# An attention stage of 24 steps, issued in the order of a table instead of step by step

## The chip, the cores and the metric

The kernel runs on one core of a Trainium2 chip. Five engines work side by side, each on its own queue of instructions and in the order of that queue: TensorE (PE in the profile; its weight loads are shown apart as PEld), VectorE (DVE), ScalarE (ACT), GpSimd (POOL) and SyncE (SP), which here issues nearly all transfers. The metric is the device time of one execution in microseconds (us); the figure for the kernel before is the median of three runs.

## The reference

Three blocks stand one behind the other. The first, on which the change works, is a linear attention with a forget gate, for 4 batches, 8 heads, 768 positions and a head size of 48:

```
f = 1 / (1 + exp(-f_logit))
for t in range(768):
    state = f[t][:, None] * state + outer(k[t], v[t])      # per batch and head, 48 x 48
    y[t]  = q[t] @ state
```

Its output, as 3072 tokens of 384 values, goes through a soft mixture of eight experts (logits against 32 slots, a softmax over tokens and one over slots, two matrices per expert with a relu between) and then through a gated block, `(sigmoid(x @ w_gate) * (x @ w_val)) @ w_out`.

## The kernel before

**Tiling.** The attention is worked in chunks of 128 positions: 6 chunks of 4 batches give 24 steps, and step i is chunk i // 4 of batch i % 4 with all eight heads (four lie side by side in the free dimension, two in the partitions). Within a step the forget gates are summed up in the logarithm, from the end of the chunk to its start, and keys and queries are scaled by the exponentials of the sums. Then scores, masked scores, output and state follow as matrix products.

**The operations of a step.** The names in brackets are those that the change's table uses, and this text uses them with the step or group behind a dot (A.4 is the scores of step 4).
- Gates, two steps together (group g holds steps 2g-1 and 2g): the transfer (F); a clamp on GpSimd (C, line 310); two activations on ScalarE, exp and ln (EX and LN, lines 314 and 315); per step the running sum, a scan on VectorE (S, line 319); two exponentials on ScalarE, with minus (E) and plus sign (R, both line 324).
- Keys and queries: one transfer for both (KQ, line 298) into one of three buffers `kq`; the key product in two halves (K, line 340) on GpSimd; the query product (Q, line 344), on GpSimd for odd steps from 3 on and on VectorE otherwise.
- State: the old one times the chunk's decay on GpSimd (SB, line 352, from step 4 on); the transposed keys by TensorE and their copy out of PSUM by ScalarE (KT and KTC, lines 156 and 157); the product of keys and values (KV, line 383) and its addition to the state on VectorE (ZA, lines 391 and 393). GG (line 350) keeps the gates' smallest values.
- Output: scores on TensorE (A, line 365); the masking on VectorE (M, line 372), which also brings them from PSUM to the one buffer `r`; query times old state (YI, line 401) and scores times values (YA, line 413) on TensorE; the copy out by ScalarE (Y, line 419).
- For the second block: the output transposed (XT, line 163) and copied (X, line 165). Once in four steps the logits of a chunk on TensorE (L), their maximum and a copy (D1), the exponentials on ScalarE (DD), a transposition (DT with the copies DTC and LNC), the running sum (SR), a product that sums up the slots' inputs (SIP, line 224) and its addition (ADD, line 233).
- For the third block: six pieces of `w_gate` and `w_val` are loaded as 64 bit numbers (RAW) and narrowed to fp32, by one ScalarE instruction (ABS, line 439) and four on VectorE (N1 to N4, lines 114 to 119), in steps 3, 6, 9, 12, 15 and 18. The experts' weights (W, 20 transfers of 768 KB, and W2) are spread over the steps by `load_weights`.

There is one PSUM buffer for the scores and one `r`, so A of a step waits for M of the step before, and M waits for YA of the step before. The buffers of keys and queries are three, so KQ.(i+3) can be issued when the last reader of step i is done.

**Order.** Nothing reorders the work: each engine takes the operations as the Python loop `for i in range(NSTEP)` issues them, with what must run ahead (gates, keys and queries of the next steps) written into the loop by hand. After the loop, a tail (from line 650) ends the last chunk, and the experts follow (`rest`).

Of the kernel before, what the change touches and what calls it, by code (L numbers as in the profile page):

```python
# [31 lines left out]
CONV_AT = 3, 6, 9, 12, 15, 18  # L32
NP2 = NSTEP // 2 + 1
LOAD_FROM, LOAD_TO = 1, NSTEP - 2
# [8 lines left out]
def body(ctx, tc, fd, kqd, v, phi, w1, w2, wg, wv, wo, out_t):  # L43
# [85 lines left out]
    def attention_in(att, aps, slow):  # L129
# [23 lines left out]
        def kt_stage(k, kts):  # L153
            ps = pt([128, HP, 112], "m", MB, "ktp")
            for h in range(HP):
                PE.transpose(ps[:, h], k[0:112, h], ident[0:112, 0:112])
            A.copy(heads_of(kts), heads_of(ps))

        def x_stage(i):
            yt = yts[i % 4]  # L160
            ps = pt([128, HP, 112], "m", MB, "xtp")
            for h in range(HP):
                PE.transpose(ps[:, h], yt[0:112, h], ident[0:112, 0:112])
            x = xt[i] = xs[i % 5]
            (V.tensor_copy if i == NSTEP - 1 else A.copy)(x, heads_of(ps))
# [37 lines left out]
        def d2(u):  # L203
            ps = pt([128, 2, T], "m", MB, "dtp")
            PE.transpose(ps[:, 0], dd, ident)
            if u < NU - 1:
                PE.transpose(ps[:, 1], ll, ident)
            A.copy(dt, ps[:, 0])
            if u < NU - 1:
                A.copy(lnat[:, u].rearrange("p b s -> p (b s)"), ps[:, 1])  # L210
# [31 lines left out]
        def fast_steps():  # L242
# [69 lines left out]
            def prep_a(g, k=None):  # L312
                w = part(g, k)
                A.activation(w, w, AF.Exp, scale=-1.0)
                A.activation(w, w, AF.Ln, bias=1.0)  # L315
# [5 lines left out]
            def prep_e(g, k=None):  # L321
                w = valid(g) if k is None else slice(k, k + 1)
                for t, sc in ((ee, -1.0), (rr, 1.0)):
                    A.activation(  # L324
                        t[g % 2][0:112, w, :, 0:T].rearrange("p k h t -> p (k h) t"),
                        part(g, k).rearrange("p (x t) -> p x t", t=T), AF.Exp, scale=sc,
                    )
# [18 lines left out]
            def z_stage(i, eng):  # L346
                g, k = at_step(i)
                if k == 1 or i == NSTEP - 1:
                    lo = max(2 * g - 1, 0)
                    eng.tensor_copy(gmin[0:112, lo:i + 1], ee[g % 2][0:112, valid(g), :, 0])  # L350
                if i >= B:
                    eng.tensor_tensor(
                        sb[i % 2][0:112], zs[i % B][0:112], decay(ee, i, 0, 1).to_broadcast([112, HP, D]),
                        op=ALU.mult,
                    )
# [15 lines left out]
            def m_stage():  # L371
# [58 lines left out]
            def load_raw(p):  # L430
                if 0 <= p < NP:
                    raws[p] = rawt[:, 0:2 * GW].rearrange("p (n w) -> p n w", w=2)
                    w, n = (wg, wv)[p // KC].bitcast(I32), 2 * GW
                    SP.dma_start(raws[p].rearrange("p n w -> p (n w)"), w[0][:, p % KC * n:(p % KC + 1) * n])

            def conv_a(i):
                if i in CONV_AT:
                    p = CONV_AT.index(i)
                    A.activation(piece(p), raws[p].bitcast(F32)[:, :, 1], AF.Abs)

            def conv(i):
                if i not in CONV_AT:
                    return [lambda: None] * 4
                p = CONV_AT.index(i)
                return narrow_steps(piece(p), raws[p])

            loads = [(768, lambda n=n: load_w1(*divmod(n, 2))) for n in range(E * 2)]
            loads += [
                (768, lambda e=e, h=h: load_w2(e, slice(4 * h, 4 * h + 4))) for e in range(2) for h in range(2)
            ]  # L450
            total, given = sum(n for n, _ in loads), [0]

            def load_weights(i, part):
                due = total * (i + part - LOAD_FROM) / (LOAD_TO - LOAD_FROM)
                while loads and given[0] < due:
                    n, f = loads.pop(0)
                    given[0] += n
                    f()

            def once(fn, i, *a):  # L460
                if 0 <= i < NSTEP:
                    fn(i, *a)

            load_f(0)
            load_f(1, 0)
            load_kq(0)
            load_phi(A)
            make_keep()
            load_f(1, 1)
            load_kq(1)  # L470
            load_v(0)
            load_f(2)
            load_v(1)
            load_kq(2)
            for t in ee + rr:
                V.memset(t[:, :, :, T:T + 1], 1.0)
            prep_c(0)
            prep_c(1, 0)
            make_identity(nc, ident)
            make_mask()  # L480
            prep_c(1, 1)
            prep_a(0)
            V.memset(aps_, 0.0)
            prep_s(0)
            prep_e(0)
            prep_a(1, 0)
            prep_k(0, V)
            prep_q(0, V)
            prep_s(1)
            V.memset(kvp[32:64], 0.0)  # L490
            PO.memset(ident0[:, 128:160], 0.0)
            for i in range(NSTEP):
                u, b = divmod(i, B)
                more = u < NU - 1
                even = i % 2 == 0
                cv = conv(i)

                if i == 0:
                    prep_e(1, 0)
                    z_stage(0, PO)  # L500
# [4 lines left out]
                if not even and (i + 5) // 2 < NP2:  # L505
                    prep_c((i + 5) // 2)
# [5 lines left out]
                if i >= 8 and b == 2 or i == 6:  # L512
                    d2b(u - 1)
                if i >= B:
                    y_inter(i)
                if i == 0:
                    kt_stage(kq[0][:, 0], kts)
                    V.memset(yps[32:64], 0.0)
                    prep_a(1, 1)
                    prep_c(2)  # L520
                once(load_kq, i + 3)
                once(load_v, i + 2)
                if i == 0:
                    load_f(3)
                if not even:
                    load_f((i + 7) // 2)
                load_raw(CONV_AT.index(i + 2) if i + 2 in CONV_AT else -1)
                load_weights(i, 0)
                if even and (i + 4) // 2 < NP2:
                    prep_a((i + 4) // 2)  # L530
                if not even or i == 0:
                    once(prep_q, i + 1, V)
                if i == 0:
                    prep_s(2)
                    prep_e(1, 1)
                if not even and (i + 3) // 2 < NP2:
                    prep_e((i + 3) // 2)

                if more:
                    kv(i)  # L540
                    z_add(i)
                if i:
                    x_stage(i - 1)
                if i + 1 < NSTEP - B:
                    kt_stage(kq[(i + 1) % 3][:, 0], kts)
                if even:
                    once(prep_s, i + 3)
                if i >= 4 and b == 0:
                    l_stage(u - 1)
                    d1(u - 1)  # L550
                if i >= 4 and b == 1:
                    d2(u - 1)
                    d1b(u - 1)
# [5 lines left out]
                if i >= 4 and b == 0:  # L559
                    d1e(u - 1)  # L560
                if i == NSTEP - 3:
                    constants()
                if i == NSTEP - 2:
                    load_w2(2, slice(0, 8))

        def slow_steps():
# [8 lines left out]
            def slow_step(i):  # L575
# [11 lines left out]
                kt_stage(kk, kts)  # L587
# [44 lines left out]
            for i in range(NSTEP):  # L632
# [4 lines left out]
                x_stage(i)  # L637
                if i % B == B - 1:
# [3 lines left out]
                    d2(u)  # L642
                    d1b(u)
# [9 lines left out]
        x_stage(NSTEP - 1)  # L653
        d1e(u)
# [6 lines left out]
        d2(u)  # L661
        t2 = pt([128, 1], "a1" if slow else "kv", name="t2")
# [402 lines left out]
```

## Time and profile before

| what | value |
|---|---|
| median of 3 runs | 385.44 us (385.29 to 385.81) |
| the profiled execution | 384.68 us, span of the core 382.9 us |
| busy in the span | PE 88%, VectorE 64%, ScalarE 55%, GpSimd 54% |
| attention, first score product to the tail | 9.27 to 138.25 us |

The span is the core's own time in the trace; every time of a row is counted from its start. The shares are means over stages with different limits: the attention uses all five engines and the transfer queue, while in the last 200 us TensorE works nearly alone at its limit. What the change does is to be read from the first 140 us. TensorE's times are modelled, because its products overlap, so a mean of a group on PE is longer than what one adds to the queue; starts can be compared.

### The profile page before, as it was taken

How to read it: one execution, taken by the hardware profiler on the slowest of the kernel's cores; microseconds unless marked ns; L12 is line 12 of the kernel's file. 1: busy time of each engine (PE TensorE's matmuls, PEld its weight loads, DVE VectorE, ACT ScalarE, POOL GpSimd, SP SyncE). 2: the span in 40 equal slices, each digit the busy share in tenths (PEclk: the TensorE clock that was granted, in tenths of full speed). 3: DMA queues.
4: the chain of work that ended last, by engine and by line, in shares of the span. 5: the costliest groups of instructions: out<-in, count | busy, mean ns of one | idle time of the engine just before them, and what ended most of it. 6: DMA issues, size and time to landing. Idle time of an engine off the chain costs nothing.

```text
span 382.9 us, 8428 instructions
## 1 busy us (share of the span) xinstructions
PE 338.7 (88%) x3406; PEld 258.0 (67%) x3406; DVE 246.9 (64%) x407; ACT 209.3 (55%) x373; POOL 207.2 (54%) x200
## 2 busy tenths in 40 slices
PE   0796969888896989995879999999999999999993
PEld 0685758676675664453558886788887887888882
DVE  5678886878888646435767765547786566444442
ACT  5676755677784421134366665666555565444440
POOL 5596855777786400002466564666555566545550
PEclk9999997999997899998699999999999999999998
DMA  7679996999997969992001240030000000222222
GB/s 265 223 243 364 360 398 228 364 391 352 386 386 258 355 231 368 415 429 109 0 0 49 118 164 3 14 153 0 0 2 1 0 2 0 82 85 82 82 85 92
DMA packets 17456, 68.33 MB, mean 178 GB/s; under 512 B 1936, under 2 KB 5376, under 8 KB 15744
## 3 DMA queue, kind: packets, MB, share of 16 engines
q1 hardware_dynamic: 17280, 67.64, 46.8%
q8 instruction: 29, 0.48, 0.5%
q14 instruction: 19, 0.16, 0.1%
q10 hardware_dynamic: 128, 0.06, 0.1%
HBM read 62.97 MB, written 4.72 MB: 177 GB/s over the span
## 4 chain that ended last, share of the span: by engine, by line


## 5 line engine op out<-in xcount | busy, mean ns | idle before, releaser
L910 POOL TENSOR_TENSOR hl<-sg,hh 128x512 fp32r<-128x512 f32 x72 | 100.8, 1400 | 77.1 <-ACT hh L908 73.6
L906 DVE TENSOR_TENSOR sg<-sg,gvp 128x512 f32<-128x512 f32 x72 | 49.5, 687 | 69.2 <-ACT sg L905 69.0
L938 PE MATMUL oup<-hh,wo 128*128 128x512 f32 x216 | 85.8, 397 | 1.4 <-ACT acc L920 1.2
L939 PE MATMUL oup<-hh,wo 128*128 128x512 f32 x216 | 84.8, 393 | 0.0
L908 ACT CAST hh<-sg 128x512 fp32r<-128x512 f32 x72 | 44.8, 622 | 55.1 <-DVE sg L906 55.1
L340 POOL TENSOR_TENSOR kq<-kq,e 112x256 f32<-112x256 f32 x46 | 39.8, 885 | 30.3 <-ACT e L324 27.7
L905 ACT ACTIVATE sg<-gvp 128x512 f32<-128x512 f32 x72 | 42.9, 596 | 17.1 <-PE gvp L900 16.9
L900 PE MATMUL gvp<-cs,gs 128*128 128x512 f32 x144 | 46.7, 406 | 5.0 <-ACT gs L891 3.4
L938 PEld LDWEIGHTS oup<-hh,wo 128*128 128x128 f32 x216 | 40.9, 189 | 12.9 <-ACT acc L920 2.1
L939 PEld LDWEIGHTS oup<-hh,wo 128*128 128x128 f32 x216 | 41.0, 190 | 8.2
L945 PE MATMUL oup<-hl,wo 128*128 128x512 f32 x162 | 46.4, 395 | 0.1
L413 PE MATMUL y<-r,v 128*48 128x128 f32 x384 | 28.8, 298 | 13.8 <-DVE r L372 13.8
L372 DVE TENSOR_TENSOR r<-a,raw 128x1024 f32<-128x1024 f32 x24 | 29.1, 1211 | 13.4 <-PE a L365 13.4
L900 PEld LDWEIGHTS gvp<-cs,gs 128*128 128x128 f32 x144 | 27.9, 194 | 12.9 <-ACT gs L891 3.8
L319 DVE TENSOR_TENSOR_SCAN f<-raw,f 112x512 f32<-112x512 f32 x24 | 31.9, 1343 | 6.6 <-ACT f L315 6.6
L945 PEld LDWEIGHTS oup<-hl,wo 128*128 128x128 f32 x162 | 30.7, 190 | 7.1 <-POOL hl L910 0.5
L413 PEld LDWEIGHTS y<-r,v 128*48 128x48 f32 x384 | 22.1, 133 | 19.2 <-DVE r L372 17.1
L365 PE MATMUL a<-kq 48*64 48x64 f32 (+1 forms) x768 | 24.2, 270 | 9.3 <-DVE kq L344 9.3
L365 PEld LDWEIGHTS a<-kq 48*64 48x64 f32 x768 | 20.3, 147 | 14.0 <-DVE kq L344 9.3
L729 POOL TENSOR_TENSOR wo<-wf,wo 128x384 fp32r<-128x384 f32 x12 | 12.1, 1009 | 25.0 <-ACT wo L726 25.0
L324 ACT ACTIVATE e<-f 112x1024 f32<-112x1024 f32 (+1 forms) x14 | 13.1, 935 | 20.6 <-DVE f L319 20.6
L419 ACT COPY yt<-y 112x512 f32<-112x512 f32 x24 | 14.2, 591 | 17.7 <-PE y L413 17.7
(152 smaller groups left out, 549.0 us busy)
## 6 DMA issues: line engine op xcount, KB each, us to landing
w<-w SPq DMA_DIRECT2D x20, 768.0 KB, 7.1
kq<-kq SPq DMA_DIRECT2D x24, 512.0 KB, 5.0
f<-f SPq DMA_DIRECT2D x10, 512.0 KB, 5.8
v<-v SPq DMA_DIRECT2D x24, 192.0 KB, 5.2
w<-w SPq DMA_DIRECT2D x3, 1536.0 KB, 7.6
w2p<-w SPq DMA_DIRECT2D x3, 1536.0 KB, 10.4
rawo<-wo SPq DMA_DIRECT2D x3, 1536.0 KB, 13.9
out_t<-os SPq DMA_DIRECT2D x17, 256.0 KB, 2.1
```

Of the source, the lines that this page charges most:

```text
L319: V.tensor_tensor_scan(w, keep[0:112, ::-1], w, 0.0, op0=ALU.mult, op1=ALU.add)
L340: eng.tensor_tensor(k[:, h], k[:, h], e[:, h, :, ::1 - 2 * h], op=ALU.mult)
L365: PE.matmul(aps_[r:r + TH, j, g, h, TH * s:T], k[d, p, r:r + TH], q[d, p, TH * s:T], start=True, stop=True, skip_group_check=True, tile_po ...
L413: PE.matmul(yps[64 * h:64 * h + D, j, 2 * (i % 2) + g], vv[:, j, c:c + D], rrs[:, j, g, h], start=(i < B and g == 0), stop=True, skip_grou ...
L900: PE.matmul(p, gs[n, k][:, o:o + 128], cs[:, u].rearrange("p b t -> p (b t)"), start=True, stop=True)
L905: A.activation(sg, ps[0], AF.Sigmoid)
L906: V.tensor_tensor(sg, sg, ps[1], op=ALU.mult)
L908: A.copy(h, sg)
L910: PO.tensor_tensor(l, sg, h.bitcast(F32), op=ALU.subtract)
L938: PE.matmul(ops[u][c], wh[q][:, fq, cc[c]], h, start=(fq == 0), stop=False)
L939: PE.matmul(ops[u][c], wl[q][:, fq, cc[c]], h, start=False, stop=False)
L945: PE.matmul(ops[u][c], wh[q][:, fq, cc[c]], l, start=False, stop=False)
```

## The change

The loop over steps is replaced by a table, `ORDER`, of some 600 tokens. A token names an operation and its step, group or piece; a dictionary `steps` maps the name to a function, and the tokens are issued one by one. All engines' instructions stay in their own queue's order, which is now that of the table. To allow this, operations that were one function become two: the transposition and its copy (KT and KTC, XT and X, DT and DTC and LNC), exp and ln (EX, LN), minus and plus exponential (E, R), GG and SB, and the four narrowing instructions. The arithmetic is the same, with one exception in where it runs: `QPOOL` puts 15 query products on GpSimd (of 11 before); VectorE keeps nine (of 13). A W token always takes the next weight load of the list, whatever its number. Two lines of the table stand for it here:

```diff
-CONV_AT = 3, 6, 9, 12, 15, 18
+QPOOL = 2, 3, 5, 6, 8, 9, 11, 12, 14, 15, 17, 18, 20, 21, 23
+ORDER = """
+F.0 MK.0 F.1.0 F.2 KQ.0 F.1.1 KQ.1 ID.0 MA.0 V.0 C.0 MY.0 KQ.2 C.1.0 EX.0 MV.0 CN.0 LN.0 V.1 C.2 EX.1.0 V.2
...
+Y.22 XT.19 W.5 DTC.4 XT.20 X.19 YI.23 X.20 YA.23 LNC.4 W.17 SIP.4 Y.23 XT.21 ADD.4 XT.22 X.21 W.13 X.22
+"""
...
-        def kt_stage(k, kts):
+        mid = {}
+
+        def kt_stage(k):
             ps = pt([128, HP, 112], "m", MB, "ktp")
             for h in range(HP):
                 PE.transpose(ps[:, h], k[0:112, h], ident[0:112, 0:112])
-            A.copy(heads_of(kts), heads_of(ps))
+            mid["k"] = ps
+
+        def kt_copy(kts):
+            A.copy(heads_of(kts), heads_of(mid.pop("k")))
...
-            for i in range(NSTEP):
...
-                once(prep_k, i + 1, PO)
-                if i and even:
-                    once(prep_q, i + 1, PO)
-                once(z_stage, i + 1, PO)
...
-                a_stage(i)
-                if not even:
-                    once(prep_s, i + 3)
-                m_stage()
...
-                conv_a(i)
-                for c in cv:
-                    c()
-                y_intra(i)
-                y_out(i)
...
+            steps = {
+                "F": load_f, "C": prep_c, "EX": prep_x, "LN": prep_l, "S": prep_s,
...
+                "K": lambda i: prep_k(i, PO if i else V), "Q": lambda i: prep_q(i, PO if i in QPOOL else V),
+                "GG": g_stage, "SB": s_stage, "A": a_stage, "M": m_stage, "YI": y_inter, "YA": y_intra, "Y": y_out,
...
+            for token in ORDER.split():
+                name, *index = token.split(".")
+                steps[name](*[int(x) for x in index])
```

Three places show how instructions move. The first is VectorE's queue around the third conversion (step 9); L114 to L119 before and L142, L143, L144 and L147 now are the four narrowing instructions, L372 and L413 the masking M, L319 and L362 the scan, L391 and L432 ZA, L344 and L386 a query product. Before:

```order
L372 TENSOR_TENSOR r<-a,raw 128x1024
L344 TENSOR_TENSOR kq_115<-kq_115,rx_121 112x512
L391 TENSOR_TENSOR raw<-sb_112,kv 112x192
L199 SCALAR_TENSOR_TENSOR srun<-srun,al,su 128x1
L114 TENSOR_SCALAR wgv_82<-wgv_82 128x512
L115 TENSOR_SCALAR wgv_82<-wgv_82 128x512
L116 SCALAR_TENSOR_TENSOR wgv_82<-raw,wgv_82 128x512
L119 SCALAR_TENSOR_TENSOR wgv_82<-raw,wgv_82 128x512
L372 TENSOR_TENSOR r<-a,raw 128x1024
```

Of the kernel now, the same conversion in the same queue, which stands between M.11 and the scan of step 17:

```order
L413 TENSOR_TENSOR r<-a,raw 128x1024
L142 TENSOR_SCALAR wgv_82<-wgv_82 128x512
L143 TENSOR_SCALAR wgv_82<-wgv_82 128x512
L386 TENSOR_TENSOR kq_115<-kq_115,rx_121 112x512
L432 TENSOR_TENSOR raw<-sb_112,kv 112x192
L144 SCALAR_TENSOR_TENSOR wgv_82<-raw,wgv_82 128x512
L413 TENSOR_TENSOR r<-a,raw 128x1024
L432 TENSOR_TENSOR raw<-sb_111,kv 112x192
L147 SCALAR_TENSOR_TENSOR wgv_82<-raw,wgv_82 128x512
L362 SCALAR_TENSOR_TENSOR f<-raw,f 112x512
```

Where four narrowing instructions stood between one M and the next, three now stand in one gap, with a query product and ZA among them, and the fourth in the next gap.

The second place is ScalarE's queue at the start: the gates' activations up to the first exponentials E and R, whose results are `e` and `rx`. Before, group 0 goes through before group 1 begins:

```order
L314 ACTIVATE f_125<-f_125 112x512
L315 ACTIVATE f_125<-f_125 112x512
L324 ACTIVATE e0_122<-f_125 112x4x128
L324 ACTIVATE rx0_120<-f_125 112x4x128
L314 ACTIVATE f_125<-f_125 112x512
L315 ACTIVATE f_125<-f_125 112x512
L324 ACTIVATE e1_123<-f_125 112x4x128
```

Now exp and ln of groups 0, of half of 1 and of 2 (the row with 1024) stand ahead of the first E:

```order
L354 ACTIVATE f_125<-f_125 112x512
L358 ACTIVATE f_125<-f_125 112x512
L354 ACTIVATE f_125<-f_125 112x512
L358 ACTIVATE f_125<-f_125 112x512
L354 ACTIVATE f_125<-f_125 112x1024
L358 ACTIVATE f_125<-f_125 112x1024
L366 ACTIVATE e0_122<-f_125 112x4x128
```

Exp and ln of group 2, which stood behind the first copy of transposed keys, have moved ahead of the first E.

The third place is TensorE's queue at the end of the attention, from step 23's query times state on (L401 and L442; `xtp` is XT, `sip` is SIP, `l` the last chunk's logits L). Before:

```order
L401 MATMUL y<-kq_116,sb_112 48x128 x8
L163 MATMUL xtp<-ident,yt_100 128x112 x4
L413 MATMUL y<-r,v_119 48x128 x8
L172 MATMUL l<-yt_98,phs 32x128
L172 MATMUL l<-yt_99,phs 32x128
```

Now:

```order
L442 MATMUL y<-kq_116,sb_112 48x128 x8
L454 MATMUL y<-r,v_119 48x128 x8
L264 MATMUL sip<-x_94,dt 32x384
L264 MATMUL sip<-x_95,dt 32x384
L264 MATMUL sip<-x_96,dt 32x384
L264 MATMUL sip<-x_97,dt 32x384
L196 MATMUL xtp<-ident,yt_99 128x112 x4
L196 MATMUL xtp<-ident,yt_100 128x112 x4
L208 MATMUL l<-yt_98,phs 32x128
```

SIP of chunk 4 and two transpositions have moved behind the last YA, ahead of the logits that begin the tail.

In SyncE's queue the last six of the 20 W loads now stand behind the last value load V.23, and all of them behind every KQ.

## Rows read from the trace of the kernel before

**Rows 1.** Windows: stretch, length, busy us of PE, PEld, DVE, ACT, POOL, clock, transfers, GB/s

```profile
33.00:136.00 103.00, 87.89 (x1849) 69.00 (x1844) 81.00 (x116) 66.25 (x121) 72.31 (x84) 0.93 0.93 348
...
70.00:120.00 50.00, 40.51 (x893) 32.20 (x892) 43.59 (x60) 33.56 (x59) 36.72 (x42) 1.00 1.00 378
...
56.00:62.00 6.00, 5.88 (x84) 4.48 (x78) 2.74 (x3) 3.34 (x5) 5.40 (x7) 0.50 0.90 350
```

**Rows 2.** Waits, 33 to 136 us: total us, times, longest us

```profile
POOL kq L340 <- ACT e L324: 20.7, 8, 4.1
...
PE y L413 <- DVE r L372: 12.1, 8, 3.3
DVE r L372 <- PE a L365: 11.3, 9, 2.1
```

**Rows 3.** Timeline of TensorE: start and us of A.4, A.5, A.6 and A.23

```profile
32.55 0.90 PE L365 MATMUL a<-kq 48*64 48x128 f32 x32
39.74 0.90 PE L365 MATMUL a<-kq 48*64 48x128 f32 x32
43.82 0.90 PE L365 MATMUL a<-kq 48*64 48x128 f32 x32
...
134.98 0.90 PE L365 MATMUL a<-kq 48*64 48x128 f32 x32
```

**Rows 4.** Narrowing instructions N1 to N4 on VectorE, 33 to 136 us

```profile
33.00:136.00 103.00, 19.11 (x24) 0.93 0.93 348
```

**Rows 5.** Groups by line, 33 to 136 us: count, busy us, mean ns, idle before

```profile
L340 POOL TENSOR_TENSOR kq<-kq,e 112x256 f32<-112x256 f32 x37 | 31.8, 880 | 23.2 <-ACT e L324 20.7 <-DMA kq<-kq 2.5
...
L352 POOL TENSOR_TENSOR sb<-raw,e 112x192 f32<-112x192 f32 x19 | 15.5, 818 | 3.5 <-DVE raw L391 3.5
...
L344 POOL TENSOR_TENSOR kq<-kq,rx 112x512 f32<-112x512 f32 x10 | 11.8, 1184 | 0.0
L310 POOL TENSOR_SCALAR f<-f 112x1024 f32<-112x1024 f32 x7 | 11.1, 1583 | 0.6
...
L344 DVE TENSOR_TENSOR kq<-kq,rx 112x512 f32<-112x512 f32 x9 | 6.4, 709 | 0.0
```

**Rows 6.** Timeline at the start: clamp and scans of group 2

```profile
12.53 3.33 POOL L310 TENSOR_SCALAR f<-f 112x1024 f32<-112x1024 f32 x1
...
18.07 2.79 DVE L319 TENSOR_TENSOR_SCAN f<-raw,f 112x512 f32<-112x512 f32 x2 [2.80 <-ACT f L315]
```

**Rows 7.** Timeline at the attention's end and at the experts' second product

```profile
131.51 0.85 PE L224 MATMUL sip<-x,dt 128*32 128x384 f32 x8
...
136.41 0.60 PE L163 MATMUL xtp<-ident,yt 112*128 112x112 f32 x4
...
138.41 1.28 SPq L101 DMA_DIRECT2D w2p<-w  x3
...
158.51 0.11 PEld L798 LDWEIGHTS op<-w2p,hT 128*32 128x32 f32 x1
```

**Rows 8.** Transfers by line: KB each, median us to landing; then the landing of `w2p`

```profile
w<-w SPq DMA_DIRECT2D x20, 768.0 KB, 7.1
kq<-kq SPq DMA_DIRECT2D x24, 512.0 KB, 5.0
...
DMA to landing us min/median/max: 6.4/10.4/13.6
```

**Rows 9.** Timeline of single operations on GpSimd, with a scan on VectorE

```profile
57.04 0.51 POOL L352 TENSOR_TENSOR sb<-raw,e 112x192 f32<-112x192 f32 x1
...
58.81 1.24 DVE L319 TENSOR_TENSOR_SCAN f<-raw,f 112x512 f32<-112x512 f32 x1
58.98 1.39 POOL L352 TENSOR_TENSOR sb<-raw,e 112x192 f32<-112x192 f32 x1
...
69.34 2.31 POOL L340 TENSOR_TENSOR kq<-kq,e 112x256 f32<-112x256 f32 x2 [0.35 <-DMA kq<-kq]
...
105.44 2.07 POOL L310 TENSOR_SCALAR f<-f 112x1024 f32<-112x1024 f32 x1
```

More of the change, by code (lines that the diff above doesn't have):

```diff
@@ L33 @@
+A.21 SB.21 X.15 LNC.3 YA.20 X.16 Q.22 K.22 W.18 YI.21 M.21 V.23 L.4 ABS.5 SB.23 SIP.3 D1.4 Y.20 K.23 YA.21 N1.5
+W.19 DD.4 N2.5 A.22 N3.5 Q.23 XT.18 W.9 M.22 YI.22 X.18 XT.17 ADD.3 X.17 A.23 Y.21 W.3 SR.4 YA.22 N4.5 DT.4 M.23
+Y.22 XT.19 W.5 DTC.4 XT.20 X.19 YI.23 X.20 YA.23 LNC.4 W.17 SIP.4 Y.23 XT.21 ADD.4 XT.22 X.21 W.13 X.22
+"""
 NP2 = NSTEP // 2 + 1
[L34 removed]
 WARM = 10, 1, 0, 0, 3, 1
@@ L163, in x_stage, with x_copy @@
                 PE.transpose(ps[:, h], yt[0:112, h], ident[0:112, 0:112])
+            mid["x", i] = ps
+        def x_copy(i):
             x = xt[i] = xs[i % 5]
-            (V.tensor_copy if i == NSTEP - 1 else A.copy)(x, heads_of(ps))
+            (V.tensor_copy if i == NSTEP - 1 else A.copy)(x, heads_of(mid.pop(("x", i))))
         def l_stage(u):
@@ L207, in d2, with dt_copy, ln_copy @@
                 PE.transpose(ps[:, 1], ll, ident)
-            A.copy(dt, ps[:, 0])
-            if u < NU - 1:
-                A.copy(lnat[:, u].rearrange("p b s -> p (b s)"), ps[:, 1])
+            mid["d"] = ps
+        def dt_copy():
+            A.copy(dt, mid["d"][:, 0])
+        def ln_copy(u):
+            A.copy(lnat[:, u].rearrange("p b s -> p (b s)"), mid["d"][:, 1])
         def d2l(u):
@@ L310, in prep_c, with prep_x, prep_l @@
                 PO.tensor_scalar(w, w, BIG, FMIN, op0=ALU.min, op1=ALU.max)
-            def prep_a(g, k=None):
+            def prep_x(g, k=None):
                 w = part(g, k)
                 A.activation(w, w, AF.Exp, scale=-1.0)
+            def prep_l(g, k=None):
+                w = part(g, k)
                 A.activation(w, w, AF.Ln, bias=1.0)
@@ L319, in prep_s, with prep_e @@
                 V.tensor_tensor_scan(w, keep[0:112, ::-1], w, 0.0, op0=ALU.mult, op1=ALU.add)
-            def prep_e(g, k=None):
+            def prep_e(g, k, t, sc):
                 w = valid(g) if k is None else slice(k, k + 1)
[L323 to L327, printed above, removed]
+                A.activation(
+                    t[g % 2][0:112, w, :, 0:T].rearrange("p k h t -> p (k h) t"),
+                    part(g, k).rearrange("p (x t) -> p x t", t=T), AF.Exp, scale=sc,
+                )
             def decay(t, i, a, b):
@@ L344, in prep_q, with g_stage, s_stage @@
                 eng.tensor_tensor(q, q, decay(rr, i, 1, T + 1), op=ALU.mult)
[L346 to L355, printed above, removed]
+            def g_stage(i):
+                g = at_step(i)[0]
+                lo = max(2 * g - 1, 0)
+                PO.tensor_copy(gmin[0:112, lo:lo + valid(g).stop - valid(g).start], ee[g % 2][0:112, valid(g), :, 0])
+            def s_stage(i):
+                PO.tensor_tensor(
+                    sb[i % 2][0:112], zs[i % B][0:112], decay(ee, i, 0, 1).to_broadcast([112, HP, D]), op=ALU.mult
+                )
             def a_stage(i):
@@ L441, in conv @@
[L441 to L466, printed above, removed]
+                raws[p] = rawt[:, 0:2 * GW].rearrange("p (n w) -> p n w", w=2)
@@ new lines, in load_raw, with conv_a, conv @@
+                w, n = (wg, wv)[p // KC].bitcast(I32), 2 * GW
+                SP.dma_start(raws[p].rearrange("p n w -> p (n w)"), w[0][:, p % KC * n:(p % KC + 1) * n])
+            def conv_a(p):
+                A.activation(piece(p), raws[p].bitcast(F32)[:, :, 1], AF.Abs)
+            def conv(p, n):
+                narrow_steps(piece(p), raws[p])[n]()
+            loads = [lambda n=n: load_w1(*divmod(n, 2)) for n in range(E * 2)]
+            loads += [lambda e=e, h=h: load_w2(e, slice(4 * h, 4 * h + 4)) for e in range(2) for h in range(2)]
@@ L467, in fast_steps @@
+            for n in range(4):
+                steps[f"N{n + 1}"] = lambda p, n=n: conv(p, n)
             load_phi(A)
             make_keep()
[L469 to L474, printed above, removed]
             for t in ee + rr:
                 V.memset(t[:, :, :, T:T + 1], 1.0)
[L477 to L481, printed above, removed]
```

120 lines of the change are left out of this document (44 added, 76 removed).

## The prediction

> **What bounds the kernel now.** I read the windows first, since the shares of the whole span mix the attention with 200 us in which TensorE is nearly alone. Between the score products of step 4 and step 23 lie 102.4 us for 19 steps, 5.39 us a step [rows 3], and in that stretch no engine is full: TensorE's modelled busy time is 87.9 of 103 us, VectorE 81.0, GpSimd 72.3, ScalarE 66.3, and the transfer engines are at 0.93 with 348 GB/s [rows 1]. So no engine's work sets the time alone; order does. The list of waits shows a ring in which each engine waits for the next: GpSimd's key products wait 20.7 us for ScalarE's exponentials, TensorE's output products 12.1 us for the masking on VectorE, and the masking 11.3 us for the scores [rows 2]. The timeline of scores tells where it opens: the step from 39.74 to 43.82 takes 4.08 us, the step before it, which has a conversion's result to wait for, 7.19 us [rows 3]. Eight of the 19 steps have neither a conversion nor a drop of TensorE's clock nor the logits of a chunk, and they run in 4.1 to 4.7 us, 4.33 in the mean. The long steps are those in which the four narrowing instructions stand between two maskings on VectorE, so that TensorE waits for `r`, and the ones that follow such a wait at half clock: from 56 to 62 us the granted clock is 0.50, the 1.2 GHz level [rows 1]; a second such stretch lies at 122 to 126 us, and both follow a wait of TensorE for `r`, of which the longest is 3.3 us [rows 2].
>
> The middle is tighter than the whole: from 70 to 120 us VectorE is busy for 43.6 of 50 us (87%) and the transfers are at 1.00 with 378 GB/s [rows 1]. There the table has less to gain than at either end.
>
> **The change, part by part.** Durations are those of the profiled execution, so the sum starts from its 384.68 us, which is 0.76 us below the median of 385.44.
>
> *The order in the 19 steps.* If every step ran as the eight undisturbed ones, the stretch would take 19 x 4.33 = 82.3 us. The conversions are 19.1 us of VectorE [rows 4]; if none of them were hidden, 82.3 + 19.1 = 101.4 us, which is nearly the 102.4 of now, so this account explains the present time. They can be hidden: without them VectorE has 81.0 - 19.1 = 61.9 us of work, less three query products at 0.71 us [rows 5], 59.8 us or 3.15 a step, and leaves 1.18 us free in a step of 4.33, 22.5 us in all against 19.1. The new queue shows them divided over the gaps between maskings, one to three at a time, beside products and ZA that wait for other engines. I take half of them as hidden, because an in-order queue never fills all gaps and because the middle is already at 87%: (82.3 + 101.4) / 2 = 91.9 us. The windows give nearly the same from another side: VectorE's 81.0 - 2.1 = 78.9 us at the 87% that it reaches from 70 to 120 us is 90.5 us. Gain 102.4 - 91.9 = 10.5 us, between 20.1 and 1.0. The half clock is inside these steps; with shorter waits TensorE loses less of it, at most the 3 us lost in those 6 us and about as much in the other stretch.
>
> *The query products.* GpSimd gets 13 in this stretch where it had 10, 3 x 1.18 = 3.6 us, and has 72.3 + 3.6 = 75.9 us to do in 91.9: hidden, with 16 us in hand. What is queued behind a query product there is the next key product, for which TensorE waits by way of the scores; with the cover gone the price is the 3.6 us.
>
> The trace shows GpSimd held up by VectorE: the decay of the state takes 0.51 us alone and 1.39 us where a scan of 1.24 us runs [rows 9]. The query products on GpSimd show nothing of this, 1.18 us in the mean of ten [rows 5], but none of them meets a scan in the old order. The Trainium skill (SBUF — State Buffer, "Who interferes with whom") says that a VectorE instruction with two SBUF inputs contends with a GpSimd instruction that reads SBUF and that the later one stands still; its page Perfetto Trace Analysis ("Optimizing Scalar/DVE Operations") draws from it that offloading between those two might not help. That speaks against these moves: by the rule the 13 products can each lose a scan's 1.24 us, 16.1 us, and GpSimd would have 92.0 us to do, just the length of the stretch forecast. By the row it has 75.9. Either way the sum stays; the rule takes the room that the second rival needs.
>
> *The start.* Group 2's clamp took 3.33 us and ended at 15.86 us, its scans ran from 18.07 to 20.86 [rows 6]; the scores of step 4 came at 32.55 [rows 3]. Now that group's load is third in the queue, its clamp third on GpSimd and its exp and ln ahead of the first E. That costs the first scores some 3 us, as K.0 stands behind exp, ln and one scan of group 2, and puts steps 2 and 3 forward, whose gates are ready when their keys arrive. I take 4 us for the scores of step 4. Bounds: 0, if the first 3 us are never regained, and 8, if steps 2 and 3 follow at 4.33 us each as soon as step 1 is done.
>
> *The end.* SIP of chunk 4 (0.85 us) and two transpositions (0.60 us each) stand now between the last YA and the last logits [rows 7], 2.05 us on the path, since the copy out of the last step covers as much of the logits before as of SIP now. Bounds 0 and 2.05; I take 2.0.
>
> *The loads.* The last six W loads, 4.7 MB, follow V.23 and are read only by the experts. At 378 GB/s they take 12.5 us, so they end some 2 us after the attention, and the three `w2p` loads queue behind them. Those are issued at 138.41, land after at most 13.6 us [rows 8], and are first read at 158.51 us [rows 7], 6.5 us later: hidden. Were the six later by more than these 6.5 us, the experts would wait for the difference. What comes after the attention moves as a whole.
>
> *Sum.* 384.68 - 10.5 - 4.0 + 2.0 = 372.2 us, and 0.76 more against the median: **372.9 us**.
>
> **Rivals.**
>
> *The three buffers of keys and queries set the pace.* KQ.(i+3) leaves when the last reader of step i is done, about 4.4 us after its scores begin (scores, masking, YA and YI in turn), takes 0.3 us to issue, 5.0 us to land [rows 8], then two halves of K at 0.88, Q at 1.18 and one clamp or decay of up to 1.6 ahead of them [rows 5]: 14.2 us for three steps, 4.74 a step, just below the 4.84 of the forecast. If landing grows to the 7.1 us that the weights show [rows 8], it is 16.3 us or 5.4 a step, and nothing is gained in the stretch. For it: the transfer engines are full from 70 to 120 us already. Against it: GpSimd waits for these loads for 2.5 us in all now [rows 5], and six weight loads leave the stretch's end of the queue. With landing at 6.3 us, half way: 15.5 / 3 = 5.17 a step, 98.2 us, a gain of 4.2; with half of the start (2) and the end's 2.0, 384.68 - 4.2 - 2.0 + 2.0 = 380.5, against the median 381.2 us.
>
> *GpSimd becomes the bound (slower).* It holds if the denser order lays its work beside scans throughout. The longest rows are 2.31 us for a pair of K, 1.39 for SB, 2.07 for a clamp [rows 9], and 1.18 + 1.24 = 2.42 for a query product that meets a scan; times 18.5 pairs, 19, 7.5 and 13 that is 42.7 + 26.4 + 15.5 + 31.5 = 116 us. It decides above 5.39 us a step, 102.4 in the stretch, so with two thirds of the way from 75.9 to 116 us. At 110 us the time is 384.68 + 7.6 - 2.0 + 2.0 = 392.3, against the median 393.0 us. Against it: 19 scans of 1.24 us are 23.6 us, a quarter of the stretch, and not every operation can meet one.
>
> *The change does not do what it says.* The order is another, but the ring of waits keeps its length: the gaps filled on VectorE make M late elsewhere, the start's 3 us stay, and the stretch gains as much as the end loses. Then it is 385 us. The 87% of the middle speak for it, the eight undisturbed steps against it.
>
> **How the numbers follow.** The forecast 0.62, the buffers 0.22, no change 0.06, GpSimd as the bound 0.10. The range goes from 364.5 (a stretch of 83.5 us, with start and end as forecast) to 383.5, beyond the buffers' 381.2 and short of no change; it leaves out about 0.18. About 0.2%, 0.8 us, is what a measurement of this kernel can tell from no change. Faster 0.84, within it 0.06, slower 0.10.
>
> **What would show it.** Right: the distance from the scores of step 4 to those of step 23 near 92 us, no two maskings more than 6 us apart, no half clock inside the stretch, VectorE's wait for scores well below 11.3 us, the scores of step 4 before 30 us. The buffers: GpSimd's wait for KQ loads grows from 2.5 us to 10 or more. GpSimd as the bound: busy over 95% of the stretch, its query products above 1.5 us in the mean. The end: some 2 us more between the last YA and the maximum of the last logits. The loads: a wait of the experts' products for `w2p` would show that cover gone. The forecast is wrong if steps without conversion become slower than 4.7 us, because then spreading the work costs what it gains.

## The result and the profile after

The kernel with the table takes 374.95 us in the median of four runs (372.89 to 375.81), against 385.37 us of the kernel before in the same session: a ratio of 0.9727 (95% interval [0.9681, 0.9774]), faster by 10.4 us. Medians and ranges here and below are over all runs of a kernel; the ratios leave out single runs more than 1.5% longer than its fastest. Its profiled execution took 375.19 us with a span of 373.4 us. The forecast of 372.9 us is off by 2.0 us.

The windows of the kernel after (columns as in [rows 1]) show the 19 steps first, then a part in which GpSimd is full, one in which TensorE's clock falls, with two microseconds inside it, and the time behind the attention:

```profile
30.00:123.00 93.00, 83.18 (x1828) 65.74 (x1828) 78.21 (x106) 62.75 (x115) 82.23 (x89) 0.96 0.95 349
...
30.00:80.00 50.00, 43.74 (x1016) 34.90 (x1016) 45.70 (x60) 38.13 (x63) 48.71 (x51) 1.00 0.98 357
84.00:96.00 12.00, 10.61 (x179) 8.63 (x180) 8.48 (x12) 7.47 (x15) 8.74 (x12) 0.72 0.78 262
...
90.00:92.00 2.00, 2.00 (x49) 1.91 (x48) 1.07 (x3) 1.96 (x4) 0.63 (x1) 0.50 0.95 339
...
130.00:164.00 34.00, 33.32 (x336) 15.64 (x338) 16.61 (x47) 9.22 (x19) 0.95 (x1) 1.00 1.00 414
```

The timeline of the same execution (start, us) has the scores of steps 0 and 4, of two steps in the middle and of step 23 (L406), the masking of step 23 (L413), the issue of `w2p`, and the experts' two products (L733 and L752):

```profile
13.37 1.56 PE L406 MATMUL a<-kq 48*64 48x128 f32 x32 [0.27 <-DVE kq L386]
...
30.06 0.90 PE L406 MATMUL a<-kq 48*64 48x128 f32 x32
...
85.37 0.90 PE L406 MATMUL a<-kq 48*64 48x128 f32 x32 [1.81 <-POOL kq L386]
...
90.74 1.56 PE L406 MATMUL a<-kq 48*64 48x128 f32 x32
...
122.13 0.90 PE L406 MATMUL a<-kq 48*64 48x128 f32 x32
...
124.53 1.22 DVE L413 TENSOR_TENSOR r<-a,raw 128x1024 f32<-128x1024 f32 x1 [1.43 <-PE y L454]
...
127.30 1.95 SPq L129 DMA_DIRECT2D w2p<-w  x3
...
135.65 2.78 PE L733 MATMUL hp<-w,siT 128*32 128x512 f32 x24
...
148.58 0.11 PEld L752 LDWEIGHTS op<-w2p,hT 128*32 128x32 f32 x1
```

Against before, the experts' first product stood at 145.58 us in this row of its timeline:

```profile
145.58 0.16 PEld L779 LDWEIGHTS hp<-w,siT 128*32 128x32 f32 x8 [0.24 <-DVE siT L689]
```

Three differences account for the gain. The scores of step 4 come 2.5 us earlier (30.06 against 32.55 in [rows 3]). From there to the scores of step 23 it takes 92.07 us instead of 102.43, 10.4 us less. From those to the experts' first product it takes 13.52 us instead of 145.58 - 134.98 = 10.60, 2.9 us more. That makes -2.5 - 10.4 + 2.9 = -10.0 us, and the experts start 9.9 us earlier. What follows takes as long as before to within half a microsecond (373.4 - 135.65 = 237.75 against 382.9 - 145.58 = 237.3).

The waits of the same stretch, 30 to 123 us (total, times, longest), answer to [rows 2]:

```profile
DVE r L413 <- PE a L406: 5.6, 5, 2.0
POOL sb L394 <- DVE raw L432: 4.9, 4, 2.8
...
POOL kq L382 <- DMA kq<-kq: 2.1, 2, 1.3
PE a L406 <- POOL kq L386: 2.1, 2, 1.8
...
PE y L454 <- DVE r L413: 1.7, 2, 1.4
```

The ring of waits is gone. GpSimd's key products no longer wait for the exponentials (20.7 us before), TensorE's YA waits 1.7 us for `r` where it waited 12.1, and the masking waits 5.6 us for scores where it waited 11.3. No wait in the list adds up to more than 5.6 us in 93.

The groups by line, 30 to 123 us, answer to [rows 5]:

```profile
L382 POOL TENSOR_TENSOR kq<-kq,e 112x256 f32<-112x256 f32 x38 | 36.5, 981 | 2.5 <-DMA kq<-kq 2.1 <-PE y L454 0.2
L362 DVE TENSOR_TENSOR_SCAN f<-raw,f 112x512 f32<-112x512 f32 x17 | 26.2, 1553 | 0.5 <-ACT f L358 0.4
L386 POOL TENSOR_TENSOR kq<-kq,rx 112x512 f32<-112x512 f32 x13 | 17.7, 1365 | 0.1
...
L386 DVE TENSOR_TENSOR kq<-kq,rx 112x512 f32<-112x512 f32 x6 | 5.3, 880 | 1.9 <-DMA kq<-kq 1.9
```

The price of the denser order stands in the means: a half of K takes 981 ns (880 before), a query product on GpSimd 1365 (1184), and a scan on VectorE 1553, where this row of the kernel before has 1301:

```profile
L319 DVE TENSOR_TENSOR_SCAN f<-raw,f 112x512 f32<-112x512 f32 x17 | 22.0, 1301 | 1.1 <-ACT f L315 1.1
```

### The profile page after: what moved, and what is told of

Its sections match the earlier page's. It is cut to its first block, busy times and chain, and to the rows that moved or that the text cites. A ratio compares the mean times of both kernels' runs of the same rounds, so it can differ in the third digit from the quotient of the medians.

```text
span 373.4 us, 8445 instructions
## 1 busy us (share of the span) xinstructions
PE 334.0 (89%) x3406; PEld 254.1 (68%) x3406; DVE 246.5 (66%) x403; ACT 209.0 (56%) x373; POOL 214.2 (57%) x204
## 3 DMA queue, kind: packets, MB, share of 16 engines
HBM read 62.97 MB, written 4.72 MB: 181 GB/s over the span
## 4 chain that ended last, share of the span: by engine, by line
## 5 line engine op out<-in xcount | busy, mean ns | idle before, releaser
L382 POOL TENSOR_TENSOR kq<-kq,e 112x256 f32<-112x256 f32 x46 | 44.1, 979 | 3.1 <-DMA kq<-kq 2.1
L362 DVE TENSOR_TENSOR_SCAN f<-raw,f 112x512 f32<-112x512 f32 x24 | 35.9, 1510 | 2.4 <-ACT f L358 2.3
L413 DVE TENSOR_TENSOR r<-a,raw 128x1024 f32<-128x1024 f32 x24 | 29.1, 1212 | 11.5 <-PE y L454 5.9
L454 PE MATMUL y<-r,v 128*48 128x128 f32 x384 | 27.7, 286 | 3.1 <-DVE r L413 1.7
L406 PE MATMUL a<-kq 48*64 48x128 f32 (+1 forms) x768 | 23.5, 264 | 3.9 <-POOL kq L386 2.1
L683 POOL TENSOR_TENSOR wo<-wf,wo 128x384 fp32r<-128x384 f32 x12 | 12.1, 1009 | 25.0 <-ACT wo L680 25.0
L454 PEld LDWEIGHTS y<-r,v 128*48 128x48 f32 x384 | 20.9, 127 | 7.0 <-issue 2.7
L406 PEld LDWEIGHTS a<-kq 48*64 48x64 f32 x768 | 20.1, 144 | 7.5 <-POOL kq L386 2.6
L186 PE MATMUL ktp<-ident,kq 112*128 112x112 f32 x80 | 13.5, 293 | 12.2 <-DVE kq L382 12.0
```

Of the source, the lines that this page charges most:

```text
L362: V.tensor_tensor_scan(w, keep[0:112, ::-1], w, 0.0, op0=ALU.mult, op1=ALU.add)
L382: eng.tensor_tensor(k[:, h], k[:, h], e[:, h, :, ::1 - 2 * h], op=ALU.mult)
L406: PE.matmul(aps_[r:r + TH, j, g, h, TH * s:T], k[d, p, r:r + TH], q[d, p, TH * s:T], start=True, stop=True, skip_group_check=True, tile_po ...
L454: PE.matmul(yps[64 * h:64 * h + D, j, 2 * (i % 2) + g], vv[:, j, c:c + D], rrs[:, j, g, h], start=(i < B and g == 0), stop=True, skip_grou ...
```

## The experiments

The reasons stood against one another as follows. Theory one is the prediction's: the table hides the narrowing instructions N1 to N4, which the loop puts into VectorE's queue ahead of a masking. Its rivals: the pace is set by the three buffers of keys and queries or by their transfers, by GpSimd, or the gain comes from where the query products run or from start and end. Each ratio is to the kernel before in the same session.

**1. `loop_newq`: only the placement of the query products, in the old loop.**

```diff
-                if i and even:
+                if i + 1 in QPOOL:
...
-                if not even or i == 0:
+                if i + 1 not in QPOOL:
```

> The old loop with the new placement alone: 15 query products on GpSimd in place of 11. Theory one (the order brings the gain, the placement is hidden in either order): within 1 us of before, 384.4 to 386.4. Theory two (the placement relieves VectorE and brings the gain itself): 4 x 0.77 us less on VectorE, 382 us or less. Theory three (GpSimd is near its limit, every product moved there costs): 4 x 1.2 us more, about 390.

Measured: 390.43 us (387.38 to 394.17), ratio 1.0133 [1.0086, 1.0180]: slower by 5 us. Its groups (0 to 140 us) and waits (33 to 140 us):

```profile
L345 POOL TENSOR_TENSOR kq<-kq,rx 112x512 f32<-112x512 f32 x15 | 21.5, 1436 | 0.0
...
POOL kq L341 <- ACT e L325: 20.2, 9, 4.7
ACT e L325 <- DVE f L320: 18.6, 7, 5.1
PE y L414 <- DVE r L373: 16.8, 9, 4.2
```

In the loop these products have no cover: the ring of waits is as long as before, and YA's wait for `r` grew from 12.1 to 16.8 us. A product on GpSimd takes 1.44 us, where [rows 5] have 1.18. So the placement by itself is a loss, and the whole gain has to come from the order.

**2 and 3. `table_oldq` and `table_noq`: the table with the old 11 products on GpSimd, and with none.**

```diff
-QPOOL = 2, 3, 5, 6, 8, 9, 11, 12, 14, 15, 17, 18, 20, 21, 23
+QPOOL = 3, 5, 7, 9, 11, 13, 15, 17, 19, 21, 23
...
+QPOOL = ()
```

> The table with the old placement, odd steps from 3 on GpSimd (11 products). The trace shows GpSimd busy for 97 to 98% from 30 to 80 us. If GpSimd bounds that stretch, four products fewer (4 x 1.34 us over the stage, about half of them in it) give 1.5 to 4 us: 371 to 373.5. If the order alone matters: 374 to 376. If VectorE bounds it, as the prediction held, 4 x 0.9 us more work there: 377 to 378.

> The table with every query product on VectorE: GpSimd has 15 x 1.34 = 20 us less to do, VectorE 15 x 0.9 = 13.5 us more, on top of 78 of 93 us. If GpSimd is the bound and VectorE has room: 368 to 372. If VectorE then becomes the bound (78 + 13 x 0.9 = 90 of 92 us, without gaps): 376 to 382.

Measured: 376.34 us (373.66 to 379.93), ratio 0.9783 [0.9735, 0.9830], and 376.94 us (374.29 to 381.45), ratio 0.9804 [0.9754, 0.9855]. Both intervals overlap that of the changed kernel (the medians differ by 1.4 and 2.0 us), so 0, 11 and 15 products on GpSimd cannot be told apart by these runs. The window of `table_noq`:

```profile
30.00:123.00 93.00, 83.85 (x1802) 65.76 (x1802) 83.55 (x117) 63.75 (x115) 68.14 (x76) 0.96 0.95 345
```

GpSimd has 14 us less to do here (68.1 against 82.2), and the scores of step 4 and 23 stand at 30.64 and 122.99 us, 92.35 apart. A full GpSimd is therefore not by itself what sets the 92 us. VectorE, with 5 us more, doesn't lengthen them either.

**4. `loop_spread`: the old loop with N3 and N4 moved behind the next step's masking.**

```diff
+                cl = conv(i - 1)[2:]
...
+                for c in cl:
+                    c()
...
-                for c in cv:
+                for c in cv[:2]:
```

> The old loop with one part of the new order alone: of the four narrowing instructions of a conversion two stay where they are and two stand behind the masking of the next step. If long gaps between two maskings are what the table removes, six conversions lose up to 1.5 us each of TensorE's wait, and the half clock behind two of them goes: 376 to 381. If the position of the conversions does not matter, since VectorE's work is the same: 384.5 to 386.5.

Measured: 383.81 us (381.58 to 387.43, twelve runs), ratio 0.9986 [0.9951, 1.0021]: no difference. To divide the narrowing instructions in this way is not enough while the rest of the order stays.

**5 and 6. `loop_noconv` and `table_noconv`: no narrowing instructions at all, in the loop and in the table.** Both leave out N1 to N4 of all six pieces (24 instructions), so the third block multiplies unnarrowed weights.

```diff
-                for c in cv:
-                    c()
...
-KTC.5 N4.0 R.4 YA.4 D1.0 RAW.1 SB.6 LN.5 F.7 YI.5 M.5 Q.6 V.7 KV.5 KQ.8 Y.4 ZA.5 YA.5 DD.0 C.6 S.10 X.2 YI.6 V.8
...
+W.2 YA.3 KTC.4 F.6 S.7 YI.4 EX.5 V.6 Q.5 KV.4 KQ.7 M.4 KT.5 Y.3 SB.5 E.4 L.0 ZA.4 K.6 A.5 ZA.3 KTC.5 R.4 YA.4
```

> The old loop without the 24 narrowing instructions on VectorE (it leaves out the narrowing of the first gate and value weights; all else is computed). The prediction's account: the conversions stand between maskings and are not hidden at all, so the scores of step 23 come 17 to 19 us sooner after those of step 4 (83 to 86 us in place of 102.4) and the time is 366 to 369. A rival, that they are half hidden already and that the steps with conversions are long for other reasons: 8 to 11 us, 374 to 378.

> The table without the same 24 instructions (it too leaves the narrowing out). If the table hides half of them, as the prediction took it: 8 to 10 us less, 365 to 367, a stretch near 83. If it hides nearly all: 0 to 3 us less, 372 to 375, and something else sets the 92 us. If VectorE's work is the bound of the stretch: 17 to 19 us less, 356 to 358.

Measured: 373.40 us for the loop in the median of four runs (371.50 to 374.14, and one of 546.48 far outside; the other three have 372.66), ratio 0.9757 [0.9649, 0.9864]; 373.24 us for the table (370.92 to 373.66), ratio 0.9732 [0.9644, 0.9820]. The loop's window, scores of steps 4, 5, 6 and 23 with the first logits (L172), and longest waits:

```profile
33.00:122.00 89.00, 82.11 (x1828) 64.34 (x1824) 64.57 (x91) 66.79 (x122) 66.84 (x84) 1.00 1.01 396
...
32.77 0.90 PE L365 MATMUL a<-kq 48*64 48x128 f32 x32
...
36.62 1.08 PE L172 MATMUL l<-yt,phs 112*32 112x128 f32 x32
...
38.64 0.90 PE L365 MATMUL a<-kq 48*64 48x128 f32 x32
42.71 0.90 PE L365 MATMUL a<-kq 48*64 48x128 f32 x32
...
121.78 0.90 PE L365 MATMUL a<-kq 48*64 48x128 f32 x32
...
DVE r L372 <- PE a L365: 18.2, 11, 2.6
POOL kq L340 <- DMA kq<-kq: 18.1, 12, 3.4
```

The table's scores of steps 4 and 23:

```profile
30.33 0.90 PE L405 MATMUL a<-kq 48*64 48x128 f32 x32
...
120.17 0.90 PE L405 MATMUL a<-kq 48*64 48x128 f32 x32
```

This pair settles the main question. Without the narrowing, loop and table take the same time. In the loop the stretch falls from 102.4 to 89.0 us, in the table only from 92.1 to 89.8. So the narrowing costs the loop 13.4 us of the stretch and the table 2.2. That difference, 11.2 us, covers the 10.4 us by which the table is shorter; without narrowing its order is 0.8 us longer than the loop's. (Each stretch is read from one execution, and whole runs of one kernel differ by 2 to 4 us, so the small figures are sizes and no more.) With the narrowing the half-clock stretches of the loop go too (1.00 throughout): they had followed waits for `r`, and their price is part of the 13.4. What then waits in the loop is GpSimd's K for its transfers, 18.1 us, at 396 GB/s.

Two things besides work done in the gaps are in these figures. In the loop N1 stands at the head of VectorE's queue while it waits for ScalarE's ABS, three times for 1.5 us, and all that follows waits with it:

```profile
DVE wgv L114 <- ACT wgv L439: 4.4, 3, 1.5
```

And the table puts four of the 24 instructions outside the stretch: N1 to N3 of the first piece run before the scores of step 3, N4 of the last behind those of step 23. In the window from 30 to 123 us, which still holds that N4, this row has VectorE's narrowing, where [rows 4] have 19.11 us for 24:

```profile
30.00:123.00 93.00, 15.74 (x21) 0.96 0.95 349
```

Outside the stretch the four cost nothing that shows either: without narrowing the table's scores of step 4 come at 30.33 us, with it at 30.06, and the experts' first product follows the scores of step 23 after 13.7 us without it (133.83 - 120.17), after 13.5 with it.

**7. `table_kq4`: a fourth buffer of keys and queries** (in a slot of the weights, for which the last two W loads then wait until step 23).

```diff
-            kq = [at([128, 2, HP, T], f"kq{i}") for i in range(3)]
+            kq = [at([128, 2, HP, T], f"kq{i}") for i in range(3)] + [slot(9, [128, 2, HP, T], "kq3")]
```

> The table with four buffers of keys and queries (the fourth lies where the last two weight loads go, so these wait for step 23). If the ring of three buffers sets the pace, the stretch of 92 us loses 4 us or more: 371 or less. If not: 374 to 376, and the wait of GpSimd and VectorE for these loads, 4.0 us in all, goes with no effect on the end.

Measured: 375.26 us (373.06 to 377.31), ratio 0.9791 [0.9674, 0.9907], and 93.0 us from the scores of step 4 to those of step 23 (31.08 and 124.11): nothing gained. The ring of buffers is not the limit.

**8. `table_late_w`: all 20 W loads at the end of the table** (one run).

```diff
-M.1 R.2 KT.2 K.3 W.0 ZA.1 YA.1 LN.3 F.5 N2.0 Q.3 A.2 N3.0 KTC.2 V.4 Y.0 Q.4 KV.2 KQ.5 C.4 Y.1 KT.3 M.2 XT.1
+M.1 R.2 KT.2 K.3 ZA.1 YA.1 LN.3 F.5 N2.0 Q.3 A.2 N3.0 KTC.2 V.4 Y.0 Q.4 KV.2 KQ.5 C.4 Y.1 KT.3 M.2 XT.1 KTC.3
```

> The table with all 20 loads of the experts' weights behind the last value load. Looked at for its stretch from the scores of step 4 to those of step 23 alone, since the experts then wait for 15.7 MB. If the transfers, at 0.95 of their time and 349 GB/s, set the 92 us: 87 us or less. If the order of the engines' work sets it: 91 to 93 us, at some 200 GB/s. The whole gets longer by the loads that are late, 15 to 30 us.

Measured: 399.75 us; the experts now wait for their weights. In the attention:

```profile
31.00:125.00 94.00, 84.57 (x1796) 67.42 (x1796) 78.96 (x104) 64.07 (x115) 81.15 (x87) 0.93 0.72 241
```

The transfers moved 241 GB/s instead of 349, and the stretch took 93.3 us (31.80 to 125.10). The clock is lower here, 0.93 in the mean against 0.96; as an estimate from these two means that is 5.6 us more at half clock, which could hide a gain of 3 us at most, not the 5 that the reason asked for. The transfers don't set the table's pace either.

**9, 10 and 11. `table_start`, `table_tail`, `table_both`: the two ends of the table.** The first puts KQ.0 ahead of F.2, and E.0, R.0, K.0 and Q.0 ahead of group 2's activations. The second reorders the last 60 tokens or so: copies and transpositions earlier, SIP.4 ahead of M.23, and the W loads last. In it and in the third X.17 stands ahead of SIP.3, which still reads its buffer, so chunk 3's slot sum takes step 17's values for step 12's.

```diff
-F.0 MK.0 F.1.0 F.2 KQ.0 F.1.1 KQ.1 ID.0 MA.0 V.0 C.0 MY.0 KQ.2 C.1.0 EX.0 MV.0 CN.0 LN.0 V.1 C.2 EX.1.0 V.2
-LN.1.0 RAW.0 S.0 EX.2 C.1.1 LN.2 S.1 E.0 S.3 R.0 GG.0 E.1.0 F.3 K.0 EX.1.1 K.1 LN.1.1 R.1.0 Q.0 KT.0 S.2 ABS.0
+F.0 MK.0 F.1.0 KQ.0 F.2 F.1.1 KQ.1 ID.0 MA.0 V.0 C.0 MY.0 KQ.2 C.1.0 EX.0 MV.0 CN.0 LN.0 V.1 C.2 EX.1.0 V.2
+LN.1.0 RAW.0 S.0 E.0 R.0 EX.2 C.1.1 LN.2 S.1 K.0 Q.0 S.3 GG.0 E.1.0 F.3 EX.1.1 K.1 LN.1.1 R.1.0 KT.0 S.2 ABS.0
...
-Y.22 XT.19 W.5 DTC.4 XT.20 X.19 YI.23 X.20 YA.23 LNC.4 W.17 SIP.4 Y.23 XT.21 ADD.4 XT.22 X.21 W.13 X.22
+A.23 Y.22 W.3 SR.4 N4.5 XT.20 X.20 YI.23 SIP.4 M.23 YA.23 Y.23 XT.21 ADD.4 XT.22 X.21 X.22 W.5 W.17 W.13
```

> The table with the old order at its very start alone: the load of the first keys ahead of group 2's gates, and the first exponentials, key and query product ahead of group 2's exp, ln and scan. The prediction counted some 3 us for the late first scores (13.4 us in the trace, 9.3 before). If they are on the path: first scores near 10.5, the later steps 2 to 3 us sooner, 372 to 373. If group 2's gates and loads set steps 2 to 4 anyway: the scores of step 4 stay within 1 us of 30.1, 374 to 376.

> The table with its last 50 tokens in another order: two of the late transpositions and the transposition of the logits stand ahead of the last scores, the masked products of step 22 ahead of the scores of step 23, the slots' sum ahead of the last masked products. The trace has 13.5 us from the last scores to the experts' first product, 10.6 before. If what stands behind the last scores is what the end lost: the start of the experts moves 1 to 2 us, 373 to 374. If TensorE's work between step 21 and the end is full in any order: within 0.5 us.

> The two changes together. If both are on the path and add up: 3 to 5 us less than the table, 370 to 372. If neither is: 374 to 376.

Measured: 374.99 us (373.58 to 377.14), ratio 0.9739 [0.9710, 0.9767]; 374.63 us (371.97 to 374.82), ratio 0.9719 [0.9687, 0.9752]; 374.33 us (371.65 to 378.06), ratio 0.9722 [0.9677, 0.9767]. None differs from the changed kernel. Of `table_start`, the scores of steps 0 and 4:

```profile
9.44 1.56 PE L406 MATMUL a<-kq 48*64 48x128 f32 x32
...
30.72 0.90 PE L406 MATMUL a<-kq 48*64 48x128 f32 x32 [0.35 <-DVE r L413]
```

The first scores come 3.9 us earlier than in the changed kernel, and those of step 4 no earlier at all: the late start costs nothing in this order. In `table_both` the experts' first product follows the scores of step 23 after 11.9 us instead of 13.5, but these 1.6 us do not appear in the median either.

**12. `table_bunched`: the table, with N1 to N4 of a piece one behind the other at N4's place.**

```diff
-KTC.5 N4.0 R.4 YA.4 D1.0 RAW.1 SB.6 LN.5 F.7 YI.5 M.5 Q.6 V.7 KV.5 KQ.8 Y.4 ZA.5 YA.5 DD.0 C.6 S.10 X.2 YI.6 V.8
+W.2 YA.3 KTC.4 F.6 S.7 YI.4 EX.5 V.6 Q.5 KV.4 KQ.7 M.4 KT.5 Y.3 SB.5 E.4 L.0 ZA.4 K.6 A.5 ZA.3 KTC.5 N1.0 N2.0
+N3.0 N4.0 R.4 YA.4 D1.0 RAW.1 SB.6 LN.5 F.7 YI.5 M.5 Q.6 V.7 KV.5 KQ.8 Y.4 ZA.5 YA.5 DD.0 C.6 S.10 X.2 YI.6 V.8
```

> The table with the four narrowing instructions of each conversion in a row again, at the place of the last of them. The table hides nearly all of the 19 us (without them it is 1 to 2 us faster, the loop 11 us). If it hides them because they are divided: 3 us or more are lost, 378 to 384. If it hides them because scores, transpositions and products of other steps stand ahead in TensorE's queue while VectorE converts: 374 to 377.

Measured: 379.90 us (377.06 to 382.38), ratio 0.9861 [0.9815, 0.9907]. The scores of steps 4 and 23:

```profile
29.76 0.90 PE L406 MATMUL a<-kq 48*64 48x128 f32 x32
...
127.39 0.90 PE L406 MATMUL a<-kq 48*64 48x128 f32 x32 [0.39 <-POOL kq L386]
```

The stretch is 97.6 us long, 5.6 more than in the changed kernel. Bunched, half of the gain is lost; divided in the old loop, nothing was won. So, as far as these two divisions show, both are needed: the rest of the order, and the division into gaps. Part of the loss may be the instructions themselves: this row has 20.1 us for 20 of them from 29 to 125 us, a mean of 1.00 where the changed kernel has 0.75. The runs don't separate the two.

```profile
29.00:125.00 96.00, 20.08 (x20) 0.96 0.88 321
```

## Why the prediction came out

**The order in the 19 steps: the number right, its two parts wrong.** Forecast 91.9 us, measured 92.07. The mechanism is shown by experiments 5 and 6: the gain is the narrowing that VectorE now does while others work, with the waits and the half clock that it brought in the loop. But the step that took half of its 19.1 us as hidden failed: in the table all but 2.2 us cost nothing. The floor failed as well: 19 undisturbed steps were put at 82.3 us, and without narrowing they take 89.0 in the loop and 89.8 in the table, 4.7 us a step. The two errors, 7 us each way, cancelled, and that the number came out is luck.

The floor's error can be read from the starts of the scores in `loop_noconv`. Five steps hold a chunk's logits, 1.08 us of TensorE (the first of them is the step from 32.77 to 38.64 us above); they take 5.10 to 5.87 us, 5.49 in the mean, and the other fourteen 3.51 to 5.83, 4.40 in the mean. The prediction left the steps with logits out of its mean and then priced all 19 by it: 5 x (5.49 - 4.33) = 5.8 of the 6.7 us that the floor was short in the loop. Why a step with logits is longer was not tested; the difference of the means, 1.09 us, is about what the logits take on TensorE. The mean of eight steps does not come out of the rows either: by the starts of the scores, ten steps of the kernel before have neither narrowing, nor half clock, nor logits, and they take 3.28 to 4.72 us, 4.22 in the mean.

That 82.3 + 19.1 came so near to the 102.4 us was therefore chance and no support. Against the same steps without narrowing, the six with a conversion are 10.8 us longer in the loop, the two at half clock 4.3, and the other eleven 1.7 shorter. So the 19.1 us of narrowing lengthened their own steps by 10.8 us only; the rest lay beside other waits already.

**The half clock was put away too early.** The prediction wanted none of it inside the stretch. It is there once: TensorE waits 1.81 us for a query product on GpSimd until 85.37 us, then the clock falls to the 1.2 GHz level (0.50 from 90 to 92 us, 0.72 in the mean from 84 to 96), and the scores at 90.74 take 1.56 us instead of 0.90. The price was small: `table_tail`, whose order is the same up to the scores of step 21, keeps a granted clock of 1.00, and from the scores of step 4 to those of step 21 it takes 82.9 us (31.49 to 114.43) against 83.7 (30.06 to 113.71). Two more signs that the prediction named were missed: two pairs of maskings are 6.2 and 7.4 us apart, where 6 was the limit, and the scores of step 4 come at 30.06 us, not before 30.

**The query products: hidden, as forecast, but for the size of GpSimd's work.** It was put at 75.9 us by the rows of the kernel before, and is 82.2; from 30 to 80 us GpSimd is busy for 48.71 of 50 us. K, Q and the scans have grown by 0.10, 0.18 and 0.25 us in the mean. The longest query product on GpSimd starts while two scans run, and one beside a masking alone is as short as before:

```profile
37.60 1.22 DVE L413 TENSOR_TENSOR r<-a,raw 128x1024 f32<-128x1024 f32 x1 [1.27 <-PE y L454]
...
37.94 1.18 POOL L386 TENSOR_TENSOR kq<-kq,rx 112x512 f32<-112x512 f32 x1
...
45.25 2.85 DVE L362 TENSOR_TENSOR_SCAN f<-raw,f 112x512 f32<-112x512 f32 x2
...
46.97 2.09 POOL L386 TENSOR_TENSOR kq<-kq,rx 112x512 f32<-112x512 f32 x1
```

The rule of the Trainium skill (SBUF — State Buffer, "Who interferes with whom"), that a VectorE instruction with two SBUF inputs contends with a GpSimd instruction that reads SBUF, agrees with these rows: a scan has both inputs in SBUF, a masking takes its scores from PSUM. The 92.0 us that the prediction worked out by it is not reached. Experiments 2 and 3 show that the placement has no effect in this order that can be measured, and experiment 1 that it costs 5 us in the old one.

**The start: 2.5 us instead of 4.** The direction held. The reason given for the loss was beside the point, since `table_start` shows that the late first scores are off the path.

**The end: 2.9 us instead of 2.0.** SIP and the two transpositions stand where they were said to. On top, step 23's masking starts at 124.53 us, 1.43 us after VectorE came free, because it needs the `r` that YA.22 reads, and that YA now stands behind the scores of step 23.

**The loads: right.** The three `w2p` loads are issued from 127.3 to 128.2 us and land within the times of the second row:

```profile
L129 SPq DMA_DIRECT2D w2p<-w x3: 328/431/1046, 127.3 to 128.2; - x3
...
DMA to landing us min/median/max: 9.1/13.0/16.1
```

That is 144.3 us at the latest, and `w2p` is first read at 148.58.

**The rivals.** The buffers as the limit fell with experiment 7 and with a wait of 2.1 us for KQ, where 10 were asked for. GpSimd as the bound came near in busy share, and fell with experiment 3.

**Open.** What sets the remaining 90 us of the stretch is not shown. For the table GpSimd, the narrowing, the buffers and the transfers are ruled out one by one, though not two at a time; in the loop without narrowing the transfers are full (1.01) and not ruled out. TensorE's modelled busy time is 81 to 85 us of the stretch in every variant of the table and in the loop without narrowing, so it is the natural candidate, but no run lightened TensorE. Nor was there a version that beat the changed kernel by more than these runs can tell.

## What to carry to other kernels

Price a long job that stands off the path by leaving it out in both orders: the difference of the two differences is what the new order is worth for that job. Whoever takes a mean over the quiet steps has to add the others back, the rare ones too. Where engines wait in a ring, a job in an in-order queue costs by what stands behind it, and here it took both a run-ahead order and a division of the job to hide it. An account that adds up to the present time is no proof of its parts, and a placement that loses in one order can be free in another.

## What was not expected of the hardware

In the first 20 us or so TensorE's score products take 1.56 us a step, and 0.90 later, without a change of shape. The products at 90.74 us took the same 1.56 at the 1.2 GHz level, but at the start, where those of step 1 run from 17.20 us, this window of the changed kernel shows a granted clock of 1.00:

```profile
16.00:19.00 3.00, 3.00 (x50) 2.50 (x48) 2.58 (x4) 2.68 (x4) 2.92 (x3) 1.00 0.80 266
```

Why is open. The kernel before has the same products in these rows of its timeline:

```profile
15.96 1.56 PE L365 MATMUL a<-kq 48*64 48x128 f32 x32
...
27.73 0.90 PE L365 MATMUL a<-kq 48*64 48x128 f32 x32
```

A query product on GpSimd takes 2.09 us at its longest in the changed kernel, with a median of 1.19 and a minimum of 1.17: a few long ones make up the rise of the mean. And behind the attention the transfers moved 414 GB/s over 34 us, more than the 349 in the attention, at a busy share of 1.00.
